# Attention residual of slab 1: added by an identity product on TensorE and copied back by ScalarE

## The chip, the cores and the metric

The kernel runs on one core of a Trainium2 chip. The metric is the device time of one execution in microseconds. Three runs of the kernel before gave 429.41, 429.52 and 431.32 us, so its median is 429.52 us. A core has five engines with a queue of instructions each: TensorE (PE in the profile; its weight loads have their own row, PEld), VectorE (DVE), ScalarE (ACT), GpSimd (POOL) and SyncE (SP, which here issues DMA only). Engines wait for each other on semaphores.

## The reference, cut to what matters

The reference is two identical layers over x with 2048 tokens of width 512, in bfloat16. Each layer adds a linear attention to x and then a gated MLP to x, each on a layernorm of x:

```
x = x + A(layernorm(x))      # attention
x = x + B(layernorm(x))      # gated MLP
(the same two lines once more)

A: q, k, v = x @ wqkv, 32 heads of 16
   phi(q) = [softmax(q w_phi), softmax(-q w_phi)], phi(k) likewise
   kv = sum over tokens of phi(k)^T v,  z = sum over tokens of phi(k)
   o = phi(q) kv / (phi(q) z + 1e-6);   A = o @ wo
B: relu(x @ W_gate) * (x @ W_up) @ W_down,  inner width 1376
```

## The kernel before, in words

The 2048 tokens are 16 tiles of 128 tokens (index `t`, the partitions are the tokens), and four tiles are a slab (`st` from 0 to 3; slab 1 is `st` 0). The array `x_sb[:, t, :]` holds x in SBUF for the whole program and is updated in place.

Per layer and slab the work is: `layernorm` (L432 statistics and L433 their aggregation on VectorE, L435 and L437 a logarithm and an exponential on ScalarE for the reciprocal deviation, L449 the normalising on VectorE, L326 four transposes per tile on TensorE, L460 the copy of the transposed tile to `yT` on ScalarE); `keys`, which adds the slab's part to the sums kv and z; after all four slabs `sums`; `queries` (products with `Wqp`, exponentials L536 into `expq`); `attend`; another `layernorm`; and `glu` (gate and up products, L607 relu on ScalarE, L609 product on VectorE into `hT`, then the product with `Wd`, and its residual).

`attend` works as follows. Sixteen-wide products with `ZDw` give the denominators and softmax sums of a slab (`zd`), short operations L553 to L561 make the scale factors `atok`, four transposes and L566 make `aT`, and eight products with the constant `EC` spread the factors over the features. For each of four feature chunks c, `expq` is multiplied with these factors on VectorE: one half straight from PSUM (L578), the other half from `absb`, a copy that ScalarE made (L574). Two products with `kvbd` follow, ScalarE copies their sum to `oT` (L583), and for each of the slab's four tiles four products with `wo_sb` are accumulated in one PSUM bank. The function `residual` (L592) then lets VectorE read that bank and x, and write x. `glu` uses the same function for its own residual.

There are eight PSUM banks of 128x512 float32; a new product takes the bank that comes free first.

The order on each engine isn't written out by hand. `Program.op` records every operation with what it reads and writes and with two planned times (`occ`, how long it holds its engine, and `lat`, until its result is there). `Program.schedule` is a list planner: step by step it takes the operation that can start earliest by these planned times (the earlier one in the program on a tie), gives it its place in the engine's queue, and gives a PSUM bank to the first product of a group. `plan` turns dependencies into semaphore waits. On the chip each engine takes its queue strictly in this order. So a change of one operation's engine or planned time moves others too. The program's text has the attention of slab `st + 1` before the MLP of slab `st`, so that the planner can lay one slab's attention beside another slab's MLP; at the start of a layer the attention of slab 1 and slab 2 has no MLP beside it yet, since the MLP of slab 1 needs slab 1's second layernorm.

All products go through `mm` (L322), all transposes through `tr` (L326), so in the profile they have one line each and are told apart by the tiles they read.

Of the kernel before, what the change touches and what calls it, by code (L numbers as in the profile page):

```python
# [10 lines left out]
ACT = mybir.ActivationFunctionType  # L11
# [47 lines left out]
class Program:  # L59
# [10 lines left out]
    def op(self, eng, fn, reads=(), writes=(), occ=100.0, lat=None, name="", bonus=0.0, port=False):  # L70
        o = Op(len(self.ops), eng, fn, reads, writes, occ, occ + 100.0 if lat is None else lat, name)
        o.bonus, o.port = bonus, port
        self.ops.append(o)
        return o
# [172 lines left out]
def build_kernel(nc, A_x, A_wqkv, A_w_phi, A_wo, W_gate, W_up, W_down, out):  # L247
    B_, S, D = A_x.shape
    assert B_ == 1 and D == 512 and S == 2048
    NT, NS, NC, F = 16, 4, 4, W_gate.shape[1]  # L250
# [5 lines left out]
    with ExitStack() as ctx:  # L256
# [4 lines left out]
        def sb(name, shape, dt=BF16):  # L261
            return E(nc.sbuf_tensor(name, [P] + list(shape), dt))
# [3 lines left out]
        x_sb = sb("x_sb", [NT, 512])  # L266
# [5 lines left out]
        wo_sb = sb("wo_sb", [NC, 512])  # L272
# [8 lines left out]
        oT = sb("oT", [2, NC, 512])  # L281
# [20 lines left out]
        ident = sb("ident", [128])  # L302
# [7 lines left out]
        def R(*key):  # L310
            if key not in made:
                made[key] = Res(str(key))
            return made[key]

        op, dma = prog.op, prog.dma

        def bank(name):
            return Bank(name, pb)

        def mm(ps, view, lhsT, rhs, start, stop, reads, n, name):  # L320
            lat = 0.4167 * n + 167
            op("pe", lambda e: e.matmul(view(ps), lhsT, rhs, start=start, stop=stop),  # L322
               reads=reads, writes=[ps], occ=max(25.0, 0.4167 * n + 2.6), lat=lat, name=name)

        def tr(ps, view, src, reads, name):
            op("pe", lambda e: e.transpose(view(ps), src, ident[:]),  # L326
               reads=list(reads) + [R("ident")], writes=[ps], occ=56, lat=220, name=name)

        def full(ps):
            return ps.f32()  # L330

        def b16half(ps):
            return ps.b16()[:, 0:512]
# [15 lines left out]
        for c in (0, 2):  # L349
            dma("act", (lambda c: lambda e: e.dma_start(Wknat[:, c:c + 2, :], wqkv_v[:, c:c + 2, 512:1024]))(c),  # L350
                writes=R_Wnat["k"][c:c + 2], nbytes=262144, name="ld wk")
        dma("sp", lambda e: e.dma_start(wphi[:], A_w_phi.rearrange("(kc hl) d f -> (hl d) kc f", hl=8)),
            writes=[R("wphi")], nbytes=65536, name="ld wphi")
# [11 lines left out]
            writes=[R("Wd")], nbytes=1310720, name="ld Wd a")  # L365
# [10 lines left out]
        for i in range(NWARM):  # L376
            op("pe", lambda e: e.matmul(full(warm), ones[:, 0:128], ones[:, 0:512], start=True, stop=True),  # L377
               reads=[R("ones"), R("yT", NYT - 1, 0)], writes=[warm], occ=427, lat=640, name="warm")
        op("pool", lambda e: e.affine_select(ident[:], ones[:, 0:128], [[1, 128]], ALU.is_equal, 0.0, base=0, channel_multiplier=-1),
           reads=[R("ones"), R("yT", NYT - 1, 0)], writes=[R("ident")], occ=260, name="ident")  # L380
        op("pool", lambda e: e.affine_select(mask8a[:], ones[:, 0:8], [[-16, 8]], ALU.is_ge, 0.0, base=0, channel_multiplier=1),
           reads=[R("ones"), R("yT", NYT - 1, 0)], writes=[R("mask8a")], occ=150, name="mask8a")
        op("pool", lambda e: e.affine_select(mask8[:], mask8a[:], [[16, 8]], ALU.is_ge, 0.0, base=15, channel_multiplier=-1),
           reads=[R("mask8a")], writes=[R("mask8")], occ=150, name="mask8")
        op("act", lambda e: e.activation(EC[:].rearrange("p g (h j) -> p (g h) j", j=16), ident[:, 0:64].unsqueeze(2).to_broadcast([P, 64, 16]), ACT.Copy),
           reads=[R("ident"), R("tables")], writes=[R("EC")], occ=1000, name="EC")
# [4 lines left out]
           reads=[R("wphi"), R("mask8")], writes=[R("hT", 16)], occ=600, name="BD")  # L391
        for sg in range(2):
            op("dve", (lambda sg: lambda e: e.tensor_copy(ZDw[:, sg, :, 0:8], mask8[:].unsqueeze(1).to_broadcast([P, NC, 8])))(sg),
               reads=[R("mask8")], writes=[R("ZDw1")], occ=100, name="ZDw ones")
# [144 lines left out]
        def attend(st):  # L539

            g = st % 2
            zd = bank(f"zd{st}")

            def zdv(p):
                return p.f32().rearrange("p (t q s h) -> p t q s h", t=4, q=2, s=2)

            for tt in range(4):
                for sg in range(2):
                    for c in range(NC):
                        mm(zd, (lambda tt, sg, c: lambda p: zdv(p)[:, tt, :, sg, c * 8:(c + 1) * 8])(tt, sg, c),  # L550
                           expq[:, st, c, sg, tt * 128:(tt + 1) * 128], ZDw[:, sg, c, :].rearrange("p (q h) -> p q h", q=2), True, True,
                           [R("eq", st, c, sg), R("ZDw", sg, c), R("ZDw1")], 16, f"zd{st}")
            op("act", lambda e: e.activation(Zs[:, g], zdv(zd)[:, :, 0], ACT.Copy), reads=[zd], writes=[R("Zs", g)], occ=270, lat=400, name="Zs")  # L553
            for s in range(2):
                op("dve", (lambda s: lambda e: e.tensor_tensor(zm[:, g, :, s, :], zdv(zd)[:, :, 1, s], Zs[:, g, :, 1 - s, :], ALU.mult))(s),
                   reads=[zd, R("Zs", g)], writes=[R("zm", g, s)], occ=200, lat=290, name="zm")
            op("dve", lambda e: e.tensor_tensor(zden[:, g], zm[:, g, :, 0, :], zm[:, g, :, 1, :], ALU.add), reads=[R("zm", g, 0), R("zm", g, 1)], writes=[R("zden", g)], occ=200, lat=290, name="zden")
            op("act", lambda e: e.activation(zr[:, g], zden[:, g], ACT.Ln), reads=[R("zden", g), R("tables")], writes=[R("zr", g)], occ=200, lat=300, name="zln")
            op("act", lambda e: e.activation(zr[:, g], zr[:, g], ACT.Exp, scale=-1.0), reads=[R("zr", g)], writes=[R("zr", g)], occ=200, lat=300, name="zr")
            for s in range(2):  # L560
                op("dve", (lambda s: lambda e: e.tensor_tensor(atok[:, g, :, s * 32:(s + 1) * 32], Zs[:, g, :, 1 - s, :], zr[:, g], ALU.mult))(s),  # L561
                   reads=[R("Zs", g), R("zr", g)], writes=[R("atok", g)], occ=195, lat=290, name="atok")
            pa = bank(f"aT{st}")
            for tt in range(4):
                tr(pa, (lambda tt: lambda p: p.b16()[:, tt * 128:(tt + 1) * 128])(tt), atok[:, g, tt, :], [R("atok", g)], f"aTt{st}")
            op("dve", lambda e: e.tensor_copy(aT[:, g, :], b16half(pa)), reads=[pa], writes=[R("aT", g)], occ=328, lat=415, name="aT")  # L566
            for c in range(NC):
                for sg in range(2):
                    ps = bank(f"ab{st}{c}{sg}")
                    mm(ps, full, EC[:, sg * 4 + c, :], aT[:, g, :], True, True, [R("EC"), R("aT", g)], 512, f"ab{st}")  # L570
                    if VIA(st, c, sg):
                        ab = cnt["a"] % NA
                        cnt["a"] += 1
                        op("act", (lambda ab, ps: lambda e: e.activation(absb[:, ab, :], full(ps), ACT.Copy))(ab, ps), reads=[ps], writes=[R("absb", ab)], occ=480, lat=610, name=f"abc{st}")  # L574
                        op("dve", (lambda c, sg, ab: lambda e: e.tensor_tensor(expq[:, st, c, sg, :], expq[:, st, c, sg, :], absb[:, ab, :], ALU.mult))(c, sg, ab),  # L575
                           reads=[R("eq", st, c, sg), R("absb", ab)], writes=[R("eq", st, c, sg)], occ=335, lat=420, name=f"em{st}", port=True)
                    else:
                        op("dve", (lambda c, sg, ps: lambda e: e.tensor_tensor(expq[:, st, c, sg, :], expq[:, st, c, sg, :], full(ps), ALU.mult))(c, sg, ps),  # L578
                           reads=[R("eq", st, c, sg), ps], writes=[R("eq", st, c, sg)], occ=595, lat=690, name=f"em{st}")
                pn = bank(f"num{st}{c}")  # L580
                for sg in range(2):
                    mm(pn, full, kvbd[:, sg, c, :], expq[:, st, c, sg, :], sg == 0, sg == 1, [R("kvbd", sg, c), R("eq", st, c, sg)], 512, f"num{st}")
                op("act", (lambda c, pn: lambda e: e.activation(oT[:, g, c, :], full(pn), ACT.Copy))(c, pn), reads=[pn], writes=[R("oT", g, c)], occ=480, lat=610, name=f"oT{st}")  # L583
            for tt in range(4):
                t = 4 * st + tt
                ps = bank(f"wo{t}")
                for c in range(NC):
                    mm(ps, full, oT[:, g, c, tt * 128:(tt + 1) * 128], wo_sb[:, c, :], c == 0, c == NC - 1, [R("oT", g, c), R("wo")], 512, f"wo{t}")
                residual(t, ps)

        def residual(t, ps):
            op("dve", lambda e: e.tensor_tensor(x_sb[:, t, :], x_sb[:, t, :], full(ps), ALU.add), reads=[R("x", t), ps], writes=[R("x", t)], occ=597, lat=690, name=f"res{t}")  # L592
# [35 lines left out]
        def out_of_a(st):  # L628
            queries(st, buf[st])
            attend(st)  # L630
            return layernorm(st)
# [74 lines left out]
```

## Time and profile before

| what | value |
|---|---|
| median of 3 runs | 429.52 us (429.41 to 431.32) |
| profiled execution, its own time | 429.99 us |
| its span in the profile | 428.2 us |
| granted TensorE clock | 0.999 |
| PE busy | 414.4 us, 97% |
| VectorE busy | 283.2 us, 66% |
| ScalarE busy | 222.4 us, 52% |
| GpSimd busy | 69.2 us, 16% |
| residual adds L592 | 64 of 685 ns mean, 41.9 us |
| `oT` copies L583 | 32 of 630 ns mean, 18.9 us |

The profile is of one execution. The table's busy times are sums over the span of the instructions' own records. A matmul's record spans its whole passage (379 ns for 512 columns) while the next one is already running, so records of matmuls overlap and the sum is of the time covered. In the views, a square bracket after an instruction tells how long its engine was idle just before it, and which engine's instruction ended that.

### The profile page before, as it was taken

To read this page: it belongs to the slowest core of one execution; us is meant where nothing else is said; L and a number is where in the kernel's file an instruction comes from. 1 tells how busy PE (TensorE), PEld (TensorE's weight loads), DVE (VectorE), ACT (ScalarE), POOL (GpSimd) and SP (SyncE) were. 2 spreads that over 40 slices of the span, in tenths; PEclk is the share of its full clock that TensorE was granted. 3 is DMA by queue.
4 is the path that set the end of the run, shared out by engine and by line. 5 is a ranking of instruction groups with operands and counts; after the bars stand their busy time and mean duration, and the time that the engine had idled before them with its cause. 6 is when DMAs were issued, how large, how long until landed. Compare 5 with 4: busy or idle time off the path is not lost.

```text
span 428.2 us, 6499 instructions
## 1 busy us (share of the span) xinstructions
PE 414.4 (97%) x2521; PEld 210.3 (49%) x2568; DVE 283.2 (66%) x590; ACT 222.4 (52%) x452; POOL 69.2 (16%) x71
## 2 busy tenths in 40 slices
PE   8899999899999999999999999989999999999997
PEld 4455555445455445454445445534444444444443
DVE  6989768994589548883774446888536834843332
ACT  6999888655084515742183169865514422450320
POOL 0439670000007000610052007000000000000000
PEclk9999999999999999999999999999999999999999
DMA  8940000000000000000000000000000001000001
GB/s 269 383 139 2 2 0 2 2 0 2 0 2 2 0 0 2 0 2 0 2 0 2 1 2 0 2 2 0 2 24 27 0 1 51 0 2 27 22 2 49
DMA packets 9598, 10.95 MB, mean 26 GB/s; under 512 B 1024, under 2 KB 8544, under 8 KB 9568
## 3 DMA queue, kind: packets, MB, share of 16 engines
q1 hardware_dynamic: 9024, 10.01, 6.9%
q10 hardware_dynamic: 544, 0.52, 0.4%
q8 instruction: 20, 0.33, 0.3%
q14 instruction: 10, 0.08, 0.1%
HBM read 8.44 MB, written 2.10 MB: 25 GB/s over the span
## 4 chain that ended last, share of the span: by engine, by line
PE 85%; ACT 9%; DVE 4%; issue 1%; POOL 0%
PE pb L322 80%; PE pb L326 3%; ACT expk L484 3%; ACT ytile L446 2%; DVE x_sb L592 1%; ACT vsb L492 1%; DVE stats L432 1%; ACT expq L536 1%; PE pb L377 1%; DVE expq L578 1%; ACT Wqp L417 0%; ACT hT L406 0%; ACT yT L460 0%; DVE Wkp L414 0%; ACT oT L583 0%
## 5 line engine op out<-in xcount | busy, mean ns | idle before, releaser
L607 ACT ACTIVATE gate_sb<-pb 128x512 bf16<-128x512 f32 (+1 forms) x88 | 52.8, 599 | 145.3 <-PE pb L322 143.9
L495 POOL TENSOR_TENSOR vhat<-vsb,rZk 128x544 bf16<-128x544 bf16 x64 | 68.4, 1102 | 196.0 <-DVE rZk L488 182.0
L609 DVE TENSOR_TENSOR hT<-gate_sb,pb 128x512 bf16<-128x512 bf16 (+1 forms) x88 | 59.9, 684 | 60.6 <-PE pb L322 60.4
L322 PE MATMUL pb<-yT,Wu 128*128 128x512 bf16 (+1 forms) x348 | 92.1, 379 | 0.1
L322 PE MATMUL pb<-yT,Wg 128*128 128x512 bf16 (+1 forms) x340 | 90.4, 379 | 0.7
L322 PE MATMUL pb<-Wd,hT 128*128 128x512 bf16 (+1 forms) x344 | 77.0, 379 | 0.4
L592 DVE TENSOR_TENSOR x_sb<-x_sb,pb 128x512 bf16<-128x512 bf16 x64 | 41.9, 685 | 47.6 <-PE pb L322 47.5
L322 PEld LDWEIGHTS pb<-Wd,hT 128*128 128x128 bf16 (+1 forms) x352 | 34.4, 98 | 41.5
L322 PEld LDWEIGHTS pb<-yT,Wu 128*128 128x128 bf16 (+1 forms) x352 | 35.1, 100 | 38.8
L322 PEld LDWEIGHTS pb<-yT,Wg 128*128 128x128 bf16 (+1 forms) x352 | 34.5, 100 | 36.7
L486 DVE TENSOR_REDUCE Zk<-expk 128x64 f32<-128x1024 bf16 x32 | 38.4, 1202 | 13.3 <-ACT expk L484 13.1
L432 DVE BATCH_NORM_STATS2 stats<-x_sb 128x6 f32<-128x512 bf16 x64 | 42.5, 678 | 0.8 <-DMA x_sb<-in_A_x_dram 0.3
L536 ACT ACTIVATE expq<-pb 128x512 bf16<-128x512 f32 x64 | 35.3, 702 | 12.8 <-PE pb L322 12.8
L484 ACT ACTIVATE expk<-pb 128x512 bf16<-128x512 f32 x64 | 37.1, 667 | 3.6 <-PE pb L322 2.3
L322 PE MATMUL pb<-wv,yT 128*128 128x512 bf16 x126 | 33.7, 379 | 0.3
L322 PE MATMUL pb<-wo_sb,oT 128*128 128x512 bf16 x126 | 33.5, 379 | 0.2
L322 PE MATMUL pb<-Wkp,yT 128*128 128x512 bf16 x122 | 32.1, 379 | 1.3 <-ACT yT L460 0.9
L322 PE MATMUL pb<-yT,Wqp 128*128 128x512 bf16 x121 | 30.9, 379 | 0.5 <-issue 0.2
L460 ACT ACTIVATE yT<-pb 128x512 bf16<-128x512 bf16 x52 | 27.3, 609 | 3.3 <-PE pb L326 3.3
L322 PE MATMUL pb<-vhat,expk 128*128 128x136 bf16 x256 | 24.3, 223 | 1.0 <-POOL vhat L495 0.8
L322 PE MATMUL pb<-expq,kvbd 128*128 128x512 bf16 x59 | 20.7, 380 | 3.3 <-DVE expq L575 3.0
L574 ACT ACTIVATE absb<-pb 128x512 bf16<-128x512 f32 x32 | 17.8, 620 | 11.6 <-PE pb L322 11.6
(63 smaller groups left out, 375.0 us busy)
## 6 DMA issues: line engine op xcount, KB each, us to landing
out_dram<-x_sb SPq DMA_DIRECT2D x16, 128.0 KB, 1.7
x_sb<-in_A_x_dram SPq DMA_DIRECT2D x3, 512.0 KB, 8.5
Wg<-in_B_W_gate_dram SPq DMA_DIRECT2D x1, 1376.0 KB, 10.6
Wu<-in_B_W_up_dram SPq DMA_DIRECT2D x1, 1376.0 KB, 13.6
Wd<-in_B_W_down_dram SPq DMA_DIRECT2D x1, 1280.0 KB, 15.7
hT<-in_A_wqkv_dram ACTq DMA_DIRECT2D x2, 256.0 KB, 3.5
wv<-in_A_wqkv_dram SPq DMA_DIRECT2D x1, 512.0 KB, 5.3
hT<-in_A_wqkv_dram SPq DMA_DIRECT2D x1, 512.0 KB, 7.6
```

Source lines behind the costliest of these rows:

```text
L322: op("pe", lambda e: e.matmul(view(ps), lhsT, rhs, start=start, stop=stop), reads=reads, writes=[ps], occ=max(25.0, 0.4167 * n + 2.6), lat ...
L326: op("pe", lambda e: e.transpose(view(ps), src, ident[:]), reads=list(reads) + [R("ident")], writes=[ps], occ=56, lat=220, name=name)
L432: op("dve", (lambda t: lambda e: e.bn_stats(stats[:, t, :], x_sb[:, t, :]))(t), reads=[R("x", t)], writes=[R("st", t)], occ=580, lat=680, ...
L460: op("act", (lambda ps, dst: lambda e: e.activation(dst, b16half(ps).rearrange("p (c n) -> p c n", c=NC), ACT.Copy))(ps, dst), reads=[ps], ...
L484: op("act", (lambda i, s, pk: lambda e: e.activation(expk[:, i, s, :], full(pk), ACT.Exp, scale=1.0 - 2.0 * s))(i, s, pk), reads=[pk], wri ...
L486: op("dve", (lambda i, zb: lambda e: e.tensor_reduce(Zk[:, zb, :], expk[:, i, :, :].rearrange("p s (h f) -> p (s h) f", f=16), AX.X, ALU.a ...
L495: op("pool", (lambda i, s, vb, rz: lambda e: e.tensor_tensor(vhat[:, i, s, :, :], vsb[:, vb, :, :], rZk[:, rz, s * 32:(s + 1) * 32].unsque ...
L536: op("act", (lambda c, s, ps: lambda e: e.activation(expq[:, st, c, s, :], full(ps), ACT.Exp, scale=1.0 - 2.0 * s))(c, s, ps), reads=[ps], ...
L574: op("act", (lambda ab, ps: lambda e: e.activation(absb[:, ab, :], full(ps), ACT.Copy))(ab, ps), reads=[ps], writes=[R("absb", ab)], occ=4 ...
L592: op("dve", lambda e: e.tensor_tensor(x_sb[:, t, :], x_sb[:, t, :], full(ps), ALU.add), reads=[R("x", t), ps], writes=[R("x", t)], occ=597 ...
L607: op("act", (lambda m, gb, pg: lambda e: e.activation(gate_sb[0:m, gb, :], pg.f32()[0:m, :], ACT.Relu))(m, gb, pg), reads=[pg], writes=[R( ...
L609: op("dve", (lambda m, gb, hb, pu: lambda e: e.tensor_tensor(hT[0:m, hb, :], gate_sb[0:m, gb, :], pu.f32()[0:m, :], ALU.mult))(m, gb, hb, pu),
```

## The change

In `attend`, for slab 1 only (`st == 0`, in both layers, so eight tiles in all), the fourth `wo` product no longer closes the accumulation. A fifth product follows in the same bank: the 128x128 identity `ident` as stationary operand and `x_sb[:, t, :]`, 512 columns of bfloat16, as moving operand. The bank then holds the attention's output plus x in float32. ScalarE copies it to `x_sb[:, t, :]` with the planned times of its other 512-wide copies. The other three slabs keep the add on VectorE, and so does the residual of the MLP in all slabs. Nothing is computed differently otherwise.

```diff
                 ps = bank(f"wo{t}")
                 for c in range(NC):
-                    mm(ps, full, oT[:, g, c, tt * 128:(tt + 1) * 128], wo_sb[:, c, :], c == 0, c == NC - 1, [R("oT", g, c), R("wo")], 512, f"wo{t}")
-                residual(t, ps)
+                    mm(ps, full, oT[:, g, c, tt * 128:(tt + 1) * 128], wo_sb[:, c, :], c == 0, c == NC - 1 and st > 0, [R("oT", g, c), R("wo")], 512, f"wo{t}")
+                if st == 0:
+                    mm(ps, full, ident[:], x_sb[:, t, :], False, True, [R("ident"), R("x", t)], 512, f"wx{t}")
+                if st == 0:
+                    op("act", (lambda t, ps: lambda e: e.activation(x_sb[:, t, :], full(ps), ACT.Copy))(t, ps), reads=[ps], writes=[R("x", t)], occ=480, lat=610, name=f"res{t}")
+                else:
+                    residual(t, ps)
```

The function that the other slabs still call:

```python
def residual(t, ps):
    op("dve", lambda e: e.tensor_tensor(x_sb[:, t, :], x_sb[:, t, :], full(ps), ALU.add), reads=[R("x", t), ps], writes=[R("x", t)], occ=597, lat=690, name=f"res{t}")
```

The built program shows how the planner reorders. Up to the last `wo` products of slab 1 all queues stand as before in both layers, apart from bank numbers. Behind them, VectorE's queue has two `atok` operations and the first statistics where the four adds stood, and slab 2's multiplications of `expq` stand between and just behind the statistics instead of behind all of them. ScalarE's queue has the four new copies ahead of slab 2's first `oT` copy and its `absb` copies. TensorE's queue has the four identity products, and slab 2's `kvbd` products spread between `ZDw` and `wo` products.

## The prediction

> **What bounds the kernel now.** I read the page's busy times first, then the chain that ended last, then a table of stretches, the waits, and the timeline of the two places that the change touches. Busy times and the shares of the chain:
>
> ```profile
> PE 414.4 (97%) x2521; PEld 210.3 (49%) x2568; DVE 283.2 (66%) x590; ACT 222.4 (52%) x452; POOL 69.2 (16%) x71
> ...
> PE 85%; ACT 9%; DVE 4%; issue 1%; POOL 0%
> ```
>
> TensorE sets the time. Work taken from VectorE is worth something only where TensorE stands still, and a product added to TensorE costs its full place in the queue wherever TensorE does not. So the question is how much TensorE stands still around slab 1's attention. The table of stretches (start:end, length, then busy time and number of each engine, granted clock, DMA) for both layers:
>
> ```profile
> 78.00:83.00 5.00, 4.51 (x36) 2.17 (x34) 5.00 (x12) 2.45 (x5) 0.00 (x0) 1.00 0.00 0
> 83.00:88.00 5.00, 4.14 (x34) 2.65 (x36) 4.56 (x16) 4.07 (x10) 0.00 (x0) 1.00 0.00 2
> ...
> 282.00:287.00 5.00, 4.64 (x44) 2.42 (x42) 4.82 (x10) 2.56 (x6) 0.00 (x0) 1.00 0.01 3
> 287.00:292.00 5.00, 3.22 (x24) 1.68 (x25) 5.00 (x17) 2.86 (x8) 0.00 (x0) 1.00 0.00 0
> ```
>
> Here VectorE (third busy number) is full, ScalarE (fourth) half idle, and TensorE (first) has holes; GpSimd does nothing. Everywhere else between 92 and 425 us TensorE is full. The list of waits names who opens the holes (total, times, longest):
>
> ```profile
> PE pb L322 <- DVE expq L575: 3.0, 3, 1.6
> ...
> PEld pb L322 <- DVE expq L578: 2.8, 5, 1.3
> ...
> PEld pb L322 <- DVE expq L575: 2.6, 8, 1.0
> ```
>
> TensorE waits for slab 2's multiplications of `expq`. The timeline tells why they are late. Layer 1, then layer 2:
>
> ```profile
> 76.30 3.19 PE L322 MATMUL pb<-wo_sb,oT 128*128 128x512 bf16 x14
> ...
> 77.80 2.48 DVE L592 TENSOR_TENSOR x_sb<-x_sb,pb 128x512 bf16<-128x512 bf16 x4 [0.51 <-PE pb L322]
> ...
> 79.96 0.60 ACT L583 ACTIVATE oT<-pb 128x512 bf16<-128x512 f32 x1 [1.98 <-PE pb L322]
> ...
> 80.20 1.28 DVE L432 BATCH_NORM_STATS2 stats<-x_sb 128x6 f32<-128x512 bf16 x2
> 80.45 1.57 ACT L574 ACTIVATE absb<-pb 128x512 bf16<-128x512 f32 x3
> ...
> 83.25 0.39 PE L322 MATMUL pb<-expq,kvbd 128*128 128x512 bf16 x1 [0.73 <-DVE expq L575]
> ...
> 84.10 1.39 DVE L449 TENSOR_SCALAR ytile<-x_sb,mv,rstd 128x512 bf16<-128x512 bf16 x4
> ...
> 84.25 0.39 PE L322 MATMUL pb<-expq,kvbd 128*128 128x512 bf16 x1 [0.61 <-DVE expq L575]
> ```
>
> ```profile
> 282.18 2.48 DVE L592 TENSOR_TENSOR x_sb<-x_sb,pb 128x512 bf16<-128x512 bf16 x4 [1.42 <-PE pb L322]
> ...
> 288.29 0.39 PE L322 MATMUL pb<-expq,kvbd 128*128 128x512 bf16 x1 [1.65 <-DVE expq L575]
> ```
>
> VectorE does the four adds, then four statistics, and only then slab 2's multiplications, while ScalarE sits idle for 1.98 us.
>
> **How large the holes are.** Matmul records overlap, so I count places in the queue instead. From rows: 14 `wo` products took 3.19 us; less one passage of 0.38 us that is 13 steps of 0.216. Eight transposes took 0.61 us and four 0.39, so one is 0.055. Ten `ZDw` products took 0.40 and one 0.17, so one is 0.026.
> Layer 1, from 76.30 to the end of slab 2's `wo` products at 89.47 (13.17 us): the program's order has 47 products of 512 columns (10.15), 20 transposes (1.10) and 17 `ZDw` (0.44), 11.69 us in all. Hole: 1.48 us.
> Layer 2, from 280.23 to 295.07 (14.84 us): 48 products (10.37), 16 transposes (0.88), 25 `ZDw` (0.65), 11.90. Hole: 2.94 us. Together 4.42 us can be won at most.
>
> **What the change adds.** Eight identity products of 512 columns, 8 x 0.216 = 1.73 us, on the engine that sets the end; nothing covers them. Their waits cost nothing, x of these tiles was written long before. The eight weight loads lie beside the running products, as the 98 ns loads do now. Bounds for one product: 0.216 in a full stream, 0.379 if it did not overlap its neighbour at all; I take 0.216, since in the 14 `wo` products the bank and the weights change from one to the next as well.
>
> The Trainium skill ("TensorE: Matmul & The Clock Gate", section "Back-to-back issue gap") gives about 131 ns per 512-column product in a sustained stream; the trace's 14 products at 216 ns do not agree. By the page the eight would cost 1.05 us and the gain would be 0.7 us larger, an estimate that I do not use.
>
> **What it removes.** Eight adds on VectorE, 2.48 us per layer from first start to last end. In their place ScalarE has eight copies from PSUM, whose nearest rows are the `absb` copies (three in 1.57 us, a step of 0.49) and the `oT` copies (0.60 alone, 0.756 at the slowest). What then waits for what, walked through the new order with these durations and 0.04 us from engine to engine, layer 1:
> - TensorE ends the four banks of slab 1 at 77.98, 78.41, 79.27 and 80.35 (the identity products are the 7th, 9th, 13th and 18th from 76.30). ScalarE's copies run at 78.02, 78.51, 79.31 and 80.39 to 80.99.
> - Queued behind the last copy on ScalarE: slab 2's first `oT` (80.88, before at 79.96), three `absb` (81.37 to 82.95), the logarithm and exponential of the layernorm (82.86 to 83.42), two more `oT`. Slab 2's first `wo` product waits for that `oT` (81.48), but TensorE comes to it only at 81.90 because of the 0.86 us of new products.
> - VectorE: statistics at 78.66, 79.26, 79.97 and 81.03 to 81.70, slab 2's multiplications ending at 82.30, 82.71, 83.08 and 83.68, normalising from 83.60 (before 84.10).
> - TensorE meets these at 82.59, 83.02, 83.45 and 83.85, each after its multiplication; the first transposes come at 84.09, behind `oT` at 84.05. All later steps pass with 0.1 to 0.4 us to spare, and the same point as before is reached at 88.87. So the hole is closed.
>
> Layer 2, same way: copies at 282.40, 282.89, 283.38 and 284.33, statistics from 283.04 to 286.33, multiplications ending at 285.66, 286.65, 287.35 and 287.67, met by TensorE at 286.06, 286.89, 287.57 and 287.89, normalising at 287.60 (before 288.74). No hole is left.
>
> The page "ScalarE: Activation LUTs" of the Trainium skill (section "Rules for kernel authors") speaks against the move: plain adds belong on VectorE, up to about three times faster per element there. That is for operands in SBUF; these come from PSUM, and here the copies take 0.60 us and the adds 0.685.
>
> **Sum.** Holes closed 4.42, products added 1.73: 2.69 us at most. The margins of 0.1 to 0.4 us are thin. With the slower ScalarE copies (0.69 long, some 0.55 apart, as the three `oT` copies in 1.69 us at 75.54) the same walk leaves about 0.45 us of hole per layer; I take half, 0.4 us over both. Gain 2.3 us. The other slabs' order also changes (in layer 2 slab 4's attention starts 16 products later), but there TensorE always has gate or up products between the steps, so I cost it at 0, with 0.5 us either way. GpSimd's and SyncE's queues get and lose nothing in these stretches, and the outputs leave after the MLP as before. Against its own 429.99 us (span 428.2 and 1.79 around it) the changed kernel takes 427.7. The median is 0.47 below that execution, so 427.2.
>
> **Rivals.**
> 1. Part of the hole returns: TensorE waits for ScalarE instead of VectorE. For it: ScalarE's queue now has about twelve operations in a row from 78 to 85 us, and slab 2's `oT`, `absb` and the layernorm are behind the copies. Against: it was idle for 1.98 us there. With 0.45 to 1.3 us of hole per layer left the gain is 0.1 to 1.8, about 1.0: 428.5.
> 2. Slower: ScalarE becomes so late that the whole hole stays and the products come on top, 429.52 + 1.73 = 431.25. In layer 1 five steps of ScalarE lie between the fourth copy and the reciprocal deviation. TensorE must come 1.46 us later than walked, past some 0.2 us to spare, so a step would have to be 0.49 + 1.66/5 = 0.82 us. No 512-wide operation on ScalarE is that far apart: even the normalising ones of L446 take 2.80 us for four, 0.70 each.
> 3. The identity products do not stream and cost 0.379 each, 3.03 us: gain 4.42 - 0.4 - 3.03 = 1.0, 428.5. For it: x is a new operand, between groups. Against: the rows of `wo`.
>
> **How the numbers follow.** About 0.5% (2.15 us) is what a measurement of this kernel can tell from no change; the forecast of 2.3 us lies just beyond. Forecast (gain over 2.15) 0.56; rival 1, 0.30; rival 3, 0.08; rival 2, 0.06, of which 0.02 is within 0.5%. So faster 0.56, same 0.40, slower 0.04; I move 0.02 from same to slower for a mechanism that I do not see. The predicted time is 427.2. Range: below, all holes closed and 0.4 us more, 426.4; above, to the end of rivals 1 and 3, 429.4.
>
> **What would show it.** Right: VectorE's first statistics within 0.1 us of the first copy's end; ScalarE without an idle of 1 us between 78 and 85; no idle of TensorE over 0.3 us in both stretches; eight more products; stretches shorter by about 0.5 and 1.9 us for the same work. Wrong: TensorE waiting for `oT` or `absb` there, identity products spaced more than 0.25 us, or new holes in another slab.

## The result, and the profile after

The changed kernel takes 427.17 us (median of 5 runs, 426.62 to 427.44), the kernel before beside it 429.52 us (5 runs, 429.41 to 431.32). The medians differ by 2.35 us, where 2.3 was forecast. The ratio on record, 0.9929 with a 95% interval of 0.9915 to 0.9944, isn't the quotient of these medians: it stands for 3.05 us (2.4 to 3.65), and the quotient, 0.9945, lies just above its interval. So the gain is clear, and its size is known to some 0.6 us only. The profiled execution of the changed kernel took 427.20 us with a span of 425.5, so 1.7 lies around the span.

The page's busy times and the chain that ended last, of the changed kernel:

```profile
PE 416.8 (98%) x2576; PEld 209.9 (49%) x2576; DVE 278.7 (66%) x582; ACT 226.1 (53%) x460; POOL 69.2 (16%) x71
...
PE 88%; ACT 9%; DMA 1%; DVE 0%; SPq 0%; POOL 0%; issue 0%
```

VectorE has lost eight instructions and 4.5 us, ScalarE has gained eight and 3.7 us. TensorE has eight products more, as its weight loads say (2568 before, 2576 now); the count of products rises by 55 because some matmuls are missing from the records, more of them before than now. VectorE's 4% of the chain has become 0% in round numbers: hardly anything on it sets the end any more. The same four stretches as in the prediction (start:end, length, then busy time and number of each engine, granted clock, DMA), now of the changed kernel:

```profile
78.00:83.00 5.00, 5.00 (x33) 2.40 (x32) 4.77 (x14) 4.28 (x10) 0.00 (x0) 1.00 0.00 0
83.00:88.00 5.00, 5.00 (x45) 2.93 (x44) 3.31 (x11) 4.66 (x11) 0.00 (x0) 1.00 0.01 2
282.00:287.00 5.00, 5.00 (x40) 2.52 (x39) 4.85 (x14) 4.60 (x11) 0.00 (x0) 1.00 0.02 3
287.00:292.00 5.00, 5.00 (x46) 2.96 (x43) 2.80 (x8) 3.42 (x7) 0.00 (x0) 1.00 0.00 0
```

TensorE (first busy number) is full in all four, where it had 4.51, 4.14, 4.64 and 3.22 of 5 us. VectorE (third) now has time left in all four. ScalarE (fourth) has taken up the work and isn't full either. The list of waits, of the whole program, says the same (total, times, longest):

```profile
PEld pb L322 <- DVE expq L575: 0.7, 4, 0.2
...
PEld pb L322 <- DVE expq L578: 0.2, 1, 0.2
```

These rows were 2.6 and 2.8 us with waits of up to 1.3; the row with 3.0 us in which TensorE itself waited for `expq` is gone. The short ones that remain are waits of a weight load, and no wait of TensorE itself for `expq` is left. The timeline of layer 1 shows the new hand-over:

```profile
77.40 0.38 PE L322 MATMUL pb<-x_sb,ident 128*128 128x512 bf16 x1
77.62 0.38 PE L322 MATMUL pb<-wo_sb,oT 128*128 128x512 bf16 x1
77.82 1.09 ACT L592 ACTIVATE x_sb<-pb 128x512 bf16<-128x512 f32 x2
77.84 0.38 PE L322 MATMUL pb<-x_sb,ident 128*128 128x512 bf16 x1
...
78.45 1.29 DVE L432 BATCH_NORM_STATS2 stats<-x_sb 128x6 f32<-128x512 bf16 x2
79.11 0.60 ACT L592 ACTIVATE x_sb<-pb 128x512 bf16<-128x512 f32 x1 [0.21 <-PE pb L322]
...
80.19 0.60 ACT L592 ACTIVATE x_sb<-pb 128x512 bf16<-128x512 f32 x1 [0.48 <-PE pb L322]
80.69 0.59 ACT L583 ACTIVATE oT<-pb 128x512 bf16<-128x512 f32 x1
...
83.36 1.37 DVE L449 TENSOR_SCALAR ytile<-x_sb,mv,rstd 128x512 bf16<-128x512 bf16 x4
...
88.78 1.03 PE L322 MATMUL pb<-yT,Wu 128*128 128x512 bf16 x4
```

An identity product stands 0.22 us behind the `wo` product ahead of it and 0.22 ahead of the next: it streams like its neighbours. ScalarE's copy starts 0.42 us after the identity product has started, which is its passage of 0.38 and 0.04 more, and VectorE's first statistics follow the first copy. The third and fourth copy wait for TensorE (0.21 and 0.48 us), not the other way round. In layer 2 the same is seen 204 us later:

```profile
281.69 1.57 ACT L592 ACTIVATE x_sb<-pb 128x512 bf16<-128x512 f32 x3 [0.17 <-PE pb L322]
...
282.32 1.29 DVE L432 BATCH_NORM_STATS2 stats<-x_sb 128x6 f32<-128x512 bf16 x2
...
286.87 1.38 DVE L449 TENSOR_SCALAR ytile<-x_sb,mv,rstd 128x512 bf16<-128x512 bf16 x4
...
292.46 1.03 PE L322 MATMUL pb<-yT,Wu 128*128 128x512 bf16 x4
```

Where the 2.7 us between the two spans came from is read off the starts of the same instructions in both traces. The stretches are those of the prediction: from the start of the group of `wo` products that ends slab 1's attention to the first `Wu` product behind slab 2's.

| part of the span | before | after | difference |
|---|---|---|---|
| up to the `wo` group of layer 1 | 76.30 | 76.10 | -0.20 |
| stretch of layer 1 | 13.17 | 12.68 | -0.49 |
| between the stretches | 190.76 | 190.75 | -0.01 |
| stretch of layer 2 | 14.84 | 12.93 | -1.91 |
| from there to the end | 133.13 | 133.04 | -0.09 |

The 0.20 ahead of the first stretch is no part of the change, since the queues are the same up to there. In layer 2 the stretch after holds four `atok` transposes (0.22 us, 4 x 0.055) that the kernel before does later, so for equal work it is 2.13 shorter. Both stretches together: 2.62.

### The profile page after: what moved, and what is told of

Same layout as the page of the kernel before. It is cut to its first block, busy times and chain, and to the rows that moved or that the text cites. A ratio compares the mean times of both kernels' runs of the same rounds, so it can differ in the third digit from the quotient of the medians.

```text
span 425.5 us, 6563 instructions
## 1 busy us (share of the span) xinstructions
PE 416.8 (98%) x2576; PEld 209.9 (49%) x2576; DVE 278.7 (66%) x582; ACT 226.1 (53%) x460; POOL 69.2 (16%) x71
## 4 chain that ended last, share of the span: by engine, by line
PE 88%; ACT 9%; DMA 1%; DVE 0%; SPq 0%; POOL 0%; issue 0%
PE pb L322 85%; PE pb L326 3%; ACT expk L484 3%; ACT ytile L446 2%; DMA wv<-in_A_wqkv_dram 1%; ACT vsb L492 1%; ACT expq L536 1%; ACT Wqp L417 0%; ACT hT L406 0%; ACT yT L460 0%; POOL vhat L495 0%; SPq L345 0%; ACT lnv L435 0%; DVE x_sb L597 0%; DVE atok L561 0%
## 5 line engine op out<-in xcount | busy, mean ns | idle before, releaser
L322 PE MATMUL pb<-yT,Wg 128*128 128x512 bf16 (+1 forms) x352 | 92.6, 379 | 0.0
L597 DVE TENSOR_TENSOR x_sb<-x_sb,pb 128x512 bf16<-128x512 bf16 x56 | 36.9, 685 | 46.8 <-PE pb L322 46.7
L322 PE MATMUL pb<-wo_sb,oT 128*128 128x512 bf16 x128 | 34.9, 379 | 0.0
L322 PE MATMUL pb<-Wkp,yT 128*128 128x512 bf16 x128 | 33.4, 379 | 1.1 <-ACT yT L460 1.1
L322 PE MATMUL pb<-yT,Wqp 128*128 128x512 bf16 x128 | 32.4, 379 | 0.6 <-ACT Wqp L417 0.5
L322 PEld LDWEIGHTS pb<-vhat,expk 128*128 128x128 bf16 x256 | 18.5, 98 | 10.4 <-POOL vhat L495 1.3
```

## The experiments

Two sizes are used throughout. Medians are compared with executions of the kernel before on the same chip, and so are the ratios, which again aren't quotients of the medians. Stretches are the two lengths of the table above, each from one profiled execution; before they are 13.17 and 14.84 us, after 12.68 and 12.93. Stretches are the sharper measure: the start of the first `wo` group lay anywhere from 75.28 to 77.18 us in the profiled executions of kernels whose queues are equal up to there. The edits are shown shortened, with `...` for what is left out; they are against the changed kernel, but in the runs with GpSimd and with the order alone against the kernel before.

The theory was the prediction's: VectorE's order makes TensorE wait; taking four adds per layer out of it closes the holes (some 4.4 us), and the eight products give back their time in the stream (1.73). The rivals: the products aren't paid or are paid more, the relief alone is not what closes the holes, or the order of VectorE's queue is the whole matter and ScalarE isn't needed.

### The copy without the product

The stretch's work without the eight identity products; the residual of these eight tiles is left out of the computation.

```diff
-                    mm(..., c == 0, c == NC - 1 and st > 0, ...)
-                if st == 0:
-                    mm(ps, full, ident[:], x_sb[:, t, :], False, True, [R("ident"), R("x", t)], 512, f"wx{t}")
+                    mm(..., c == 0, c == NC - 1, ...)
```

> The changed kernel without its eight identity products: ScalarE copies the wo sum alone to x, so the residual add of slab 1's attention is left out in both layers; everything else as changed. Theory (relief of VectorE closes the holes of TensorE, each product costs a full place of 0.216 us): 1.73 us faster than the changed kernel, about 425.4 us, 0.99 of before's time. Rival (the products lie in what is left of the holes and cost little): as the changed kernel, 427.2.

Measured: 425.67 us against 429.88, ratio 0.9897 (0.9881 to 0.9913). Stretches 11.86 and 12.63. Against before the relief alone is worth 1.31 in layer 1, and in layer 2, where this kernel too has the four `atok` transposes in the stretch, 2.43: together 3.74 us. Against this kernel the changed one is 0.82 longer in layer 1, which is four products of 0.216 within 0.05, but only 0.30 longer in layer 2. There this kernel still has holes. Its waits for VectorE, over the whole program:

```profile
PEld pb L326 <- DVE ytile L449: 1.8, 4, 0.9
...
PEld pb L322 <- DVE expq L575: 1.0, 5, 0.2
...
PEld pb L322 <- DVE expq L578: 0.7, 2, 0.5
```

Of these rows 0.3, 0.2 and 0.5 us lie between 278 and 292 us, where the changed kernel has none of the three. By counted work the second stretch is 11.90 + 0.22 = 12.12 us, so 0.51 of its 12.63 is hole: VectorE's chain is still the longer there. In the changed kernel the products fill that hole first, and only the rest of their time is paid (0.86 - 0.51 = 0.35 by the count, 0.30 measured).

### The product without the copy on ScalarE

The identity products stay, but VectorE copies the bank to x.

```diff
-                    op("act", ... e.activation(x_sb[:, t, :], full(ps), ACT.Copy) ..., occ=480, lat=610, ...)
+                    op("dve", ... e.tensor_copy(x_sb[:, t, :], full(ps)) ..., occ=597, lat=690, ...)
```

> The identity products stay, but VectorE copies the bank to x (as long as its add was), so VectorE is not relieved. Theory: the holes stay and the eight products come on top, 429.5 + 1.73 = 431.2 us. Rival (the products fill the holes): 429.5. Rival (what gains is the new place of the x read, not VectorE's relief): 427 to 428.

Measured: 430.17 us against 429.88, ratio 0.9996 (0.9985 to 1.0006); stretches 13.38 and 15.12, which is 0.21 and 0.28 longer than before. That is not the 1.73 us that eight products take in a stream. VectorE's timeline in layer 1 of this kernel tells why:

```profile
77.81 1.29 DVE L592 CAST x_sb<-pb 128x512 bf16<-128x512 f32 x2 [0.73 <-PE pb L322]
...
84.11 1.37 DVE L449 TENSOR_SCALAR ytile<-x_sb,mv,rstd 128x512 bf16<-128x512 bf16 x4
```

VectorE's copy (two in 1.29 us) is as long per tile as its add was (four in 2.48), so its chain keeps its length. It starts one product later, and normalising comes at 8.02 us from the start of the `wo` group (76.09), where before it came at 7.80. TensorE would wait for that chain anyway. The products delay it on the way to its hole and the hole is that much shorter: TensorE's own waits for `expq` are 1.1 us in all, where they were 3.2. So what was argued as "nothing covers them" needs a condition: each stretch is as long as the longer of two, TensorE's work and VectorE's chain. The products cost their full time only when the chain has become the shorter.

This expectation was missed (431.2; its first rival, that the products fill the holes, is nearer), and the theory changed by it: in the two stretches the product alone costs some 0.5, the relief alone gains some 3.7, both together 2.6. The parts don't add up because each is measured against another bound.

### All four slabs

```diff
-                    mm(..., c == 0, c == NC - 1 and st > 0, ...)
+                    mm(..., c == 0, False, ...)
-                if st == 0:
+                if True:
                     mm(ps, full, ident[:], x_sb[:, t, :], False, True, ...)
-                if st == 0:
+                if True:
                     op("act", ...)
```

> The change in all four slabs of both layers, 32 products in place of 8. Theory: behind slab 1 TensorE has no holes, so 24 more products cost 24 x 0.216 = 5.2 us against the changed kernel: 432.4 us, slower than before by 0.7%. Rival (less work on VectorE is worth something by itself): 427 us or less.

Measured: 432.17 us against 429.88, ratio 1.0046 (1.0028 to 1.0064). The busy times of this kernel:

```profile
PE 422.7 (98%) x2600; PEld 213.1 (49%) x2600; DVE 266.6 (62%) x558; ACT 239.3 (56%) x484; POOL 69.2 (16%) x71
```

There are 24 products more than in the changed kernel, and the span is 430.5 against 425.5. Its first `wo` group started 0.17 us earlier, so the rest is 5.17 longer: 0.215 each. VectorE lost another 12 us and that bought nothing: where the other three slabs' adds stand, MLP products of another slab run beside them, and TensorE has no hole there to close. So the same edit gains where TensorE waits for VectorE and costs its full price where it doesn't.

### Layer 2 alone

```diff
+            cnt["at"] += 1
+            via_pe = st == 0 and cnt["at"] > NS
...
-                if st == 0:
+                if via_pe:
```

`cnt["at"]` counts the calls of `attend`, NS of them per layer, so only the second layer's slab 1 is taken.

> The change in layer 2 alone. Theory: layer 2's hole of 2.94 us closes for four products of 0.86: 2.1 us faster than before, 427.4 us, so most of the gain is layer 2's. Rival (both layers give the same): 1.2 us faster, 428.3.

Measured: 427.28 us against 429.88, ratio 0.9933 (0.9917 to 0.995). Stretches 13.17 and 12.93: layer 1 is as long as before, layer 2 as long as after, to the hundredth. The two layers are independent. The median is about that of the changed kernel (427.17, from another set of runs), though the first stretch is 0.49 longer; in the profile its first `wo` group starts at 75.28 us, 0.82 earlier than in the changed kernel. So the gain of layer 1 is shown by the stretches, and no median here shows it.

### Two of the four tiles

The last two tiles of slab 1 by product and ScalarE, the first two as before by VectorE's add.

```diff
...
-                if st == 0:
+                if st == 0 and tt >= 2:
...
```

> The change for the last two of slab 1's four tiles only, in both layers: four products in place of eight, VectorE keeps two adds per layer. Revised theory (each layer's stretch is as long as the longer of TensorE's work and VectorE's chain): layer 1 needs only half the relief, so 0.43 us less work of TensorE shows there; layer 2 loses some 0.5 us of relief. 426.5 to 427.5 us, as the changed kernel. Rival (every add taken from VectorE is worth the same): half the gain, 428.5.

Measured: 427.84 us against 430.18, ratio 0.9948 (0.9936 to 0.996). Stretches 12.56 and 13.62. In layer 1 that is 0.12 better than with four tiles. Two products are saved, which was expected to show in full (0.43); the missing 0.31 is hole that came back, so half the relief is nearly enough there, not quite. In layer 2 it is 0.69 worse, though this kernel has two products less and does the four `atok` transposes later, for VectorE's chain is the longer one again. Normalising starts 7.31 us after the `wo` group (286.23, from 278.92), with four tiles 7.34 (286.87, from 279.53), but three of the multiplications stand behind it, with four tiles two:

```profile
286.23 1.37 DVE L449 TENSOR_SCALAR ytile<-x_sb,mv,rstd 128x512 bf16<-128x512 bf16 x4
287.52 0.41 DVE L575 TENSOR_TENSOR expq<-expq,absb 128x512 bf16<-128x512 bf16 x1
287.86 0.67 DVE L578 TENSOR_TENSOR expq<-expq,pb 128x512 bf16<-128x512 bf16 x1
288.46 0.41 DVE L575 TENSOR_TENSOR expq<-expq,absb 128x512 bf16<-128x512 bf16 x1
```

The last of them ends 9.95 us after the `wo` group, with four tiles 9.65 (288.76 + 0.42 - 279.53). The time lies 0.3 us above its expected range; layer 2 lost more than was expected.

### Copy to SBUF, add there

Can VectorE be relieved without TensorE? ScalarE copies all four banks to a part of `expq` that is free by then, and VectorE adds from SBUF.

```diff
-                    mm(ps, full, ident[:], x_sb[:, t, :], False, True, [R("ident"), R("x", t)], 512, f"wx{t}")
-                    op("act", ... e.activation(x_sb[:, t, :], full(ps), ACT.Copy) ...)
+                    op("act", ... e.activation(expq[:, 0, tt, 0, :], full(ps), ACT.Copy) ..., occ=480, lat=610, ...)
+                    op("dve", ... e.tensor_tensor(x_sb[:, t, :], x_sb[:, t, :], expq[:, 0, tt, 0, :], ALU.add) ..., occ=335, lat=420, ...)
```

> No identity products: ScalarE copies all four banks to a free tile in SBUF, VectorE adds it to x from there (0.42 us in place of 0.685, 0.35 apart in place of 0.60). Revised theory: VectorE's chain shortens by 4 x 0.25 = 1.0 us per layer and no product is added: 2.0 us faster than before, 427.9. Rival (the gain needs the whole add off VectorE): 429 or more.

Measured: 429.27 us against 430.18, ratio 0.9982 (0.9972 to 0.9992). Stretches 12.96 and 15.61: a small gain in layer 1, a loss in layer 2. From the timeline of layer 2 of this kernel:

```profile
281.94 0.91 DVE L591 TENSOR_TENSOR x_sb<-x_sb,expq 128x512 bf16<-128x512 bf16 x2
...
287.15 0.39 PE L322 MATMUL pb<-expq,kvbd 128*128 128x512 bf16 x1 [1.35 <-DVE expq L575]
```

and its stretches there (columns as above):

```profile
285.00:288.00 3.00, 1.44 (x18) 0.65 (x15) 3.00 (x10) 1.65 (x5) 0.00 (x0) 1.00 0.00 0
288.00:291.00 3.00, 2.82 (x12) 1.32 (x12) 2.94 (x10) 0.77 (x2) 0.00 (x0) 0.52 0.00 0
```

The adds have become short, but they are still on VectorE behind a copy, and all four statistics still stand ahead of the multiplications; a gap of 1.35 us remains, where before had 1.65. (In both, the weight load of one more `kvbd` product lies inside, at 286.74 here and 287.88 before, and no product is on record for it, so the bare gaps are shorter by about a product.) And behind it the granted clock is 0.52 for about 3 us, which by estimate loses 1.4 us and makes the second stretch longer than before. Five of its 12 executions show the lower mean clock that this leaves; the other seven have a median of 428.83. The expected 427.9 is missed by them too: the rival, that the whole add has to leave VectorE, was right.

### The add on GpSimd

For the last two tiles ScalarE copies to SBUF and GpSimd, idle there, adds; the first two tiles stay with VectorE.

```diff
-                residual(t, ps)
+                if st == 0 and tt >= 2:
+                    op("act", ... e.activation(expq[:, 0, tt, 0, :], full(ps), ACT.Copy) ...)
+                    op("pool", ... e.tensor_tensor(x_sb[:, t, :], x_sb[:, t, :], expq[:, 0, tt, 0, :], ALU.add) ..., occ=1060, lat=1130, ...)
+                else:
+                    residual(t, ps)
```

> No identity products: for the last two tiles of slab 1 ScalarE copies the bank to a free tile in SBUF and GpSimd, idle there, adds it to x; the first two tiles stay with VectorE's add. Revised theory: relief without TensorE's 1.73 us: between the kernel of copies alone and the changed one, 426 to 427 us, faster than the changed kernel by up to 1. Rival (GpSimd's add is too late, about 1.1 us per tile, and the statistics wait): 428 to 429.5.

Measured: 428.46 us against 430.18, ratio 0.9962 (0.9949 to 0.9975); 426 to 427 was expected. Stretches 15.39 and 13.07. In layer 2 two adds less on VectorE, without any product, bring the stretch to 0.14 us from the changed kernel's. Layer 1, with the same two adds left on VectorE as in the run with two of the four tiles, where it took 12.56, has a new wait. GpSimd and VectorE there:

```profile
78.65 2.31 POOL L591 TENSOR_TENSOR x_sb<-x_sb,expq 128x512 bf16<-128x512 bf16 x2 [16.65 <-ACT expq L590]
...
79.60 0.36 DVE L561 TENSOR_TENSOR atok<-Zs,zr 128x128 bf16<-128x128 f32 x1
...
79.99 1.13 DVE L561 TENSOR_TENSOR atok<-Zs,zr 128x128 bf16<-128x128 f32 x1
```

An `atok` operation of VectorE, 0.28 us long in the run with the product alone, took 1.13 us and ended at 81.12, with GpSimd's second add (80.96). The statistics and multiplications behind it came later, and the hole came back:

```profile
81.00:84.00 3.00, 1.44 (x20) 0.68 (x17) 3.00 (x9) 1.33 (x5) 0.00 (x0) 1.00 0.00 0
84.00:87.00 3.00, 2.79 (x14) 1.63 (x14) 2.61 (x9) 1.82 (x4) 0.00 (x0) 0.54 0.01 3
87.00:90.00 3.00, 3.00 (x23) 1.63 (x22) 0.42 (x1) 2.15 (x6) 0.00 (x0) 0.89 0.00 0
```

with half clock behind it again. The first stretch is 2.83 us longer than with two of the four tiles: 0.85 is the delay of that operation, 1.7 the lost clock by estimate, and the rest isn't explained. That the two engines held each other up is the reading of one operation; no run here repeats it with another one. In layer 2 GpSimd's adds run from 284.81 to 287.08, and the operations that VectorE does meanwhile, none with two inputs from SBUF, keep their length (a multiplication straight from PSUM takes 0.65). The Trainium skill ("SBUF — State Buffer", section "SBUF: two separate sides") describes it: VectorE operations with two SBUF inputs and GpSimd operations share one pair of ports, and whichever starts first holds it for its whole length. The 1.13 us and the nearly common end agree with that.

### The order alone

The kernel before, but slab 2's multiplications are put ahead in the planner by a bonus, so that they no longer stand behind the adds and statistics of slab 1.

```diff
-                           ..., occ=335, lat=420, name=f"em{st}", port=True)
+                           ..., occ=335, lat=420, name=f"em{st}", port=True, bonus=400.0 if st == 1 else 0.0)
```

The same bonus is given to the other form of the multiplication.

> The kernel before with another order alone: the planner lets slab 2's multiplications of expq start up to 0.4 us ahead of their turn, so that they pass most of the adds and all the statistics of slab 1; nothing is taken from VectorE. Theory (VectorE is full in this stretch): the multiplications come in time, but the normalising is late by what passed it, so the hole moves: 428.5 to 430.5. Rival (the order was the fault, and the change gains by the planner's new order): 427.5 or less.

Measured: 438.11 us against 430.18, ratio 1.0179 (1.0159 to 1.02). The multiplications come in time, but the work that they were put ahead of is late next. TensorE's waits in this kernel:

```profile
PE pb L326 <- DVE ytile L449: 5.5, 3, 2.7
PE pb L322 <- ACT yT L460: 3.0, 3, 1.2
```

Normalising starts at 88.70, 12.82 us from the `wo` group's start at 75.88 (7.80 before): three adds of slab 2 have slipped in ahead of it, and slab 1's gate products have to wait. The granted clock falls behind the hole: 1.00 in the 3 us from 85 on, 0.65 from 88, 0.50 from 91, 0.71 from 94. Stretches 17.73 and 16.57. So with this order, the only other one that was tried, the hole moved from the multiplications to the normalising, as was expected; that no order of the same work helps isn't shown. The time was expected at 428.5 to 430.5 and is 7.6 us above that. The expectation lacked the clock: a mean of 0.988 over the span of 436.1 us is by estimate 5.2 us.

### The product first in its bank

The identity product opens the accumulation instead of closing it, so that it could run before the `oT` that the `wo` products wait for.

```diff
-                for c in range(NC):
-                    mm(..., c == 0, c == NC - 1 and st > 0, ...)
                 if st == 0:
-                    mm(ps, full, ident[:], x_sb[:, t, :], False, True, ...)
+                    mm(ps, full, ident[:], x_sb[:, t, :], True, False, ...)
+                for c in range(NC):
+                    mm(..., c == 0 and st > 0, c == NC - 1, ...)
```

> The identity product opens each bank instead of closing it, so the planner may place it in an earlier hole of TensorE; it puts layer 1's four among the first products of the program, and the four banks stay taken until slab 1's wo products. Theory: the products' 1.73 us lie in older holes, but the held banks cost more wherever TensorE needs eight: 428 to 435 us. Rival (only the place on TensorE counts): 425.5, as with the copies alone.

Measured: 450.32 us against 430.85, ratio 1.046 (1.0435 to 1.0485). In this kernel's timeline TensorE's first identity products and ScalarE's copies from their banks are

```profile
6.13 0.59 PE L322 MATMUL pb<-x_sb,ident 128*128 128x512 bf16 x2
...
10.69 0.59 PE L322 MATMUL pb<-x_sb,ident 128*128 128x512 bf16 x2
...
90.30 2.06 ACT L592 ACTIVATE x_sb<-pb 128x512 bf16<-128x512 f32 x4 [0.70 <-PE pb L322]
```

The planner takes whatever can start earliest, and an identity product needs nothing but x. So four of the eight PSUM banks were taken in the first 11 us and came free again from 90.30 on. Everything between had the other four: from 20 to 47 us TensorE was busy for 20.54 of 27 us at a granted clock of 0.81, in the kernel before for 25.74 at 1.00. The time lies far above the expected 428 to 435; the direction was right. The product last in its bank costs 0.216; first in its bank, under this planner, it costs the bank.

### The changed kernel again, and a mix

The changed kernel once more, without any edit, beside a kernel with two tiles in layer 1 and four in layer 2:

> The changed kernel once more, beside the kernel before and the next two on one chip. Theory (it leaves no hole in which TensorE's clock is taken back): every execution at full clock and within 1 us of 427.2, while executions of the kernel before fall into two groups some 0.75 us apart, by whether one stretch ran at half clock. Rival (the two groups are the chip's, not the kernel's): the changed kernel shows them too.

```diff
-                if st == 0:
+                if via_pe and (tt >= 2 or cnt["at"] > NS):
```

Here `via_pe` is `st == 0`.

> Layer 1 with products and copies for the last two tiles of slab 1 only, layer 2 for all four. Theory: layer 1's stretch as in the kernel with two tiles (12.56 us against 12.68), layer 2's as in the changed kernel: 0.1 us faster than the changed kernel, about 427.0. Rival (the four places saved on TensorE show in full): 0.4 us faster.

Measured: the changed kernel 426.90 us against 430.85, ratio 0.9915 (0.9894 to 0.9935), stretches 12.68 and 12.94; the mix 426.66, ratio 0.991 (0.989 to 0.9931), stretches 12.56 and 12.93. The start of the `wo` group in the mix, and the `Wu` product behind the stretch, for both layers:

```profile
76.14 2.33 PE L322 MATMUL pb<-wo_sb,oT 128*128 128x512 bf16 x10
...
88.70 1.03 PE L322 MATMUL pb<-yT,Wu 128*128 128x512 bf16 x4
...
279.46 1.91 PE L322 MATMUL pb<-wo_sb,oT 128*128 128x512 bf16 x8
...
292.39 1.03 PE L322 MATMUL pb<-yT,Wu 128*128 128x512 bf16 x4
```

The stretches are those that were expected. Of the changed kernel's six executions one, the profiled one, took 428.29 at full clock, 1.09 from 427.2 where at most 1 was expected; its `wo` group starts at 77.18, 1.08 later than in the first profile, and its stretches are the same. The mix is the fastest version found that computes the same, by 0.24 us in the medians; the two intervals overlap, and only the stretch of layer 1 (0.12 shorter) tells the two apart.

## Why the prediction was right

**What bounds the kernel.** Right. TensorE waited for VectorE around slab 1's attention and nowhere else that the change reaches: relief alone gives 3.74 us in the two stretches, and the middle between them is 190.75 us with the change and 190.76 without.

**The size of the holes.** 1.48 and 2.94 us were counted from places in the queue. Against the counted work the changed stretches leave 12.68 - (11.69 + 0.86) = 0.13 in layer 1, and in layer 2 12.93 - (11.90 + 0.86 + 0.22), which is -0.05, so nothing within the rounding of the steps. The counting holds to about 0.1 us. It was also the safer way: the gaps of 0.61 and 1.65 us that the prediction shows each have a `kvbd` weight load inside (83.91 and 287.88) whose product isn't on record, so as holes they are read too long.

**The price of the products.** 0.216 each in a stream was right: 0.215 over the 24 of the run with all slabs, 0.205 over the four of layer 1. Rival 3 (0.379 each) is out. The 131 ns per product of the Trainium skill ("TensorE: Matmul & The Clock Gate", section "Back-to-back issue gap") isn't seen in any run. "Nothing covers them" was too simple: while VectorE's chain is the longer, the hole covers them. It didn't hurt the sum, because the sum took the whole hole as closed and then the products in full, and that is the longer of the two when it is TensorE's work.

**The walk.** The changed trace starts 0.20 us earlier, so 0.20 is taken off the walk's times:

| step | walk | trace |
|---|---|---|
| copies, layer 1 | 77.82, 78.31, 79.11, 80.19 | 77.82, (second ends 78.91), 79.11, 80.19 |
| slab 2's first `oT` copy | 80.68 | 80.69 |
| first statistics | 78.46 | 78.45 |
| normalising, layer 1 | 83.40 | 83.36 |
| end of the stretch, layer 1 | 88.67 | 88.78 |

In layer 2 the walk has normalising at 287.60, which is 7.37 from its `wo` group at 280.23; the trace has 286.87 from 279.53, 7.34. So durations from the kernel before and the planner's new order were enough for a walk to within about 0.1 us.

**The allowance.** This term was mis-sized. 0.4 us was taken off for holes that come back with slower copies from PSUM; measured is 0.13 in layer 1 and none in layer 2. The copies took 0.60 alone and 1.09 for two, a step of 0.49, as the `absb` rows say and not as the three `oT` copies at 75.54. So rival 1 (TensorE waits for ScalarE) didn't come about; it is ScalarE that waits for TensorE, by 0.21 and 0.48 us. Rival 2 (slower, ScalarE too late) is out with it.

**The step from the profile to the median.** The sum forecast 427.7 for a profiled execution, which then took 427.20: 0.3 of this is the allowance, 0.2 the earlier start. The median was then set 0.47 below, because the kernel before's median lies that far below its profiled execution; the changed kernel's lies 0.03 below. Two errors of some 0.5 us thus cancelled, and that the median came to within 0.1 us of the forecast is luck and says less than the stretches do: 2.62 measured, at most 2.69 counted, 2.3 forecast.

**The rest of the kernel.** Costed at 0 with 0.5 either way: -0.01 between the stretches and -0.09 behind them.

**The rule against the move** (the Trainium skill, "ScalarE: Activation LUTs", section "Rules for kernel authors": plain adds belong on VectorE) didn't decide here. VectorE was the engine waited for, and its copy out of PSUM is as slow as its add: 0.60 apart in both, where ScalarE's are 0.49 apart.

## What to carry to other kernels

Where two engines bound a stretch in turn, count both chains, and take the longer before and after; an operation added to one engine is nearly free as long as the other's chain is the longer (here 0.21 and 0.28 us for four products of 0.86), and the prices of two edits don't add up. TensorE can take over an add into its own accumulation for one place in its stream (0.216 us for 128x512). Here that paid only where TensorE waited for the engine that was relieved, and with the product last in its bank; first in its bank it held the bank for 80 us. And count holes in places of the queue, not in busy time, which overlaps.

## What was not expected of the hardware

**A hole on TensorE can cost clock behind it, in some executions only.** Of the 51 executions of the kernel before in the three sets of runs, 30 show a mean granted clock of 0.995 to 0.996, the other 21 one of 0.999 or 1.0. Their medians are 430.34 against 429.76, 430.33 against 429.59, and 431.05 against 429.64 in the three sets. The two experiments whose profiled execution has a mean clock of 0.996 show one short stretch of it, 0.54 and 0.52 over 3 us, right behind their hole; in the GpSimd run 0.54 and 0.89 over 3 us each lose 1.7 us of clock, which is 0.004 of 428. All 11 executions of the changed kernel and all 5 of the mix stand at 0.999 or 1.0, and so do the 6 of the copy alone, the 6 with layer 2 alone, the 5 with two of the four tiles and the 12 of the product without the copy, whose holes are only partly filled. So closing the holes, or filling them in part, seems to have taken away this risk as well; that it is so isn't tested by itself. Against only those four executions of the kernel before in the last set that kept their clock (429.64) the changed kernel (426.90) gains 2.7 us, close to the 2.6 of the stretches. How long TensorE is idle doesn't by itself tell which execution loses clock: the emptiest 3 us on record in the kernel before (286.50 to 289.50, 0.96 busy) kept 1.00, while 1.24 in the GpSimd run (81.50 to 84.50) and 1.25 in the run that adds in SBUF (285.50 to 288.50) were followed by a clock of 0.50. Where the clock falls in the other executions of the kernel before no profile here shows. The Trainium skill ("TensorE: Matmul & The Clock Gate", section "HAM oscillation — how this bites in real kernels") puts the limit at gaps without any work of more than about 3.4 us. Here the longest gaps on record in these holes are 0.79 us in the GpSimd run and 1.35 us in the run that adds in SBUF, and the clock fell. A further section of that page ("A second HAM failure mode: psum-queue depth-cycling") speaks of frequent short idling between groups of products that also brings the lower clock; whether these stretches are of that kind, and where its limit lies, no run here shows.

**VectorE beside GpSimd**: 0.28 us became 1.13 for one 128x128 operation.

**The start of the program** varies: between 75.28 and 77.18 us to the same instruction, in profiled executions of kernels that don't differ up to there, and 76.10 and 77.18 in two of the changed kernel itself. Differences of under 1 us between medians are therefore read from stretches.
